# GEGLU feed-forward on one core: the head's first loads on one queue, ScalarE's table load ahead of its DMA

## The chip, the core and the metric

The kernel runs on one core of a Trainium2 chip. A core has five engines with their own instruction streams: TensorE (PE, matrix products), VectorE (DVE), ScalarE (ACT), GpSimd (POOL) and SyncE (SP, here only issuing DMAs). DMAs are issued by SP and by ACT, each onto a queue of its own; the packets of both queues run on the core's 16 DMA engines. The metric is device time in microseconds (us), median over runs.

## The reference

```python
B, S, D, F = 32, 32, 1024, 3584          # x: 1024 rows of 1024; all bfloat16
return (gelu(x @ w_gate) * (x @ w_up)) @ w_down      # gelu: tanh form
```

With the 32 x 32 rows flattened, x is 1024x1024, w_gate and w_up are 1024x3584 and w_down is 3584x1024.

## The kernel before

**The work.** Both layers are done with Strassen's scheme (seven products of half-size blocks in place of eight, in Winograd's form). In the first layer x is cut into two halves of rows (512 tokens each) and two halves of its 1024 inner columns; held transposed on the chip, these are the tiles `b11`, `b12`, `b21`, `b22`, each 128 partitions x 4 row blocks x 512 tokens. A row block is 128 of the inner dimension. The weights are cut likewise, and their sums (`s1` to `s4`, mostly on GpSimd) and the sums of x (`t1` to `t4`, on VectorE) feed the products. A main loop goes over 14 chunks of 256 columns of the gate and up weights; the second layer follows with the same scheme.

**The head.** Sums of weights and of x need many loads, so the kernel starts with products that need no sums: the second half of the gate's inner dimension (gate row blocks 4 to 7, called k = 0 to 3 here) times `b21`, for the first 24 column tiles. They come in groups of four column tiles, `a12_ahead[i]` (i = 0 to 5), 512 columns each; the first two groups are called `a12a`, the others `a12b`. TensorE's order here is written out by hand (`tc.manual_schedule()`), and each engine runs its instructions in that order:

1. six warm-up products on constants (line 256);
2. `transposed(0)`: x's first needed row block is loaded as it lies (`x_nat`), four TensorE transposes (line 264) turn it, and two VectorE copies (line 267) bring it into `b21` row block 0;
3. the products (line 284) of group i = 0 with k = 0, first half of the tokens, then `transposed(1)` for `b21` row block 1, then the second half of k = 0, and k = 1;
4. group i = 1 with k = 0 and 1 (eight products of 512 columns);
5. group i = 0 with k = 2 and 3, then group i = 1 with k = 2 and 3. `b21` row blocks 2 and 3 don't pass through TensorE: one transposing DMA from SP brings them (`load_xT(0, KD + KQ, DT)`, line 218). Then the groups i = 2, 3, 4 and so on.

**The loads that feed it**, in the order of their queues (line 197 is `load_nat`, one row block of x, 128 KB; line 211 is `load_ahead(i, k0, k1)`, row blocks k0 to k1 of group i, 128 KB each):

- SP: `x_nat` block 0; group 0, k = 0; group 0, k = 1; the transposing DMA; group 0, k = 2 and 3; group 1, k = 2 and 3; the halves of groups 2 and 3; the first chunk's weights; and more.
- ACT: `probe`, a fetch of 0.1 KB out of the gate rows of k = 0 and 1 (line 207); `x_nat` block 1; group 1, k = 0 and 1 (256 KB). Then ScalarE's first instruction that computes, a GELU on one column (line 248), which is preceded by the load of its function table. ScalarE then waits for the first products to copy out of PSUM.

**The completion counters.** The framework gives each DMA that SP or ACT issues one of eight completion semaphores, in turn, over both queues together, in the order in which the framework comes to the DMAs. A DMA that gets a semaphore that an earlier one holds carries a wait for that one's landing; the issuing engine stands at the instruction until then. In the kernel before, the eight semaphores go, in order, to `probe`, `x_nat` block 0, `x_nat` block 1, group 0 with k = 0, group 0 with k = 1, group 1 with k = 0 and 1, the transposing DMA, and group 0 with k = 2 and 3; SP's next DMA (group 1, k = 2 and 3) is the first with such a wait, for `probe`.

Of the kernel before, what the change touches and what calls it, by code (L numbers as in the profile page):

```python
# [13 lines left out]
def kernel(  # L14
# [20 lines left out]
    nc = tc.nc  # L35
    P = nc.NUM_PARTITIONS
    fp32 = mybir.dt.float32
    f32r = mybir.dt.float32r
    bf16 = mybir.dt.bfloat16
# [10 lines left out]
    KD = DT // 2  # L50
# [4 lines left out]
    KQ = DT // 4  # L55
# [8 lines left out]
    wg_r = w_gate.rearrange("(dt dp) f -> dp dt f", dp=P)  # L64
# [8 lines left out]
    xpool = one.enter_context(tc.tile_pool(name="x", bufs=1))  # L73
# [33 lines left out]
    def acc(tag):  # L107
        return ps1.tile([P, NB], fp32, name=f"ps{tag}", tag=tag, bufs=BANKS[tag])
# [82 lines left out]
    NB_P = NB // P  # L191
# [3 lines left out]
    with tc.manual_schedule():  # L195
        def load_nat(eng, dt, p0, p1):
            eng.dma_start(  # L197
                out=x_nat[:, p0:p1, dt * P : (dt + 1) * P],
                in_=xf[p0 * P : p1 * P, (KD + dt) * P : (KD + dt + 1) * P].rearrange("(b p) d -> p b d", p=P),
            )  # L200
# [1 line left out]
        assert KQ == 2  # L202
        load_nat(nc.sync, 0, 0, NB_P)


        probe = xpool.tile([P // 8, KQ, 2], bf16, name="probe")
        nc.scalar.dma_start(out=probe, in_=wg_r[::8, KD : KD + KQ, :2])

        def load_ahead(i, k0, k1, eng=nc.sync):
            f0 = i * KB  # L210
            eng.dma_start(
                out=a12_ahead[i][:, k0:k1, :],
                in_=wg_r[:, KD + k0 : KD + k1, f0 * P : (f0 + KB) * P],
            )

        def load_xT(nb, d0, d1):
            t = ((b11, b12), (b21, b22))[d0 // KD][nb]
            nc.sync.dma_start_transpose(
                out=t[:, d0 % KD : (d1 - 1) % KD + 1, :], in_=xf[nb * NB : (nb + 1) * NB, d0 * P : d1 * P]
            )  # L220

        load_ahead(0, 0, 1)
        load_nat(nc.scalar, 1, 0, NB_P)
        load_ahead(0, 1, 2)
        load_xT(0, KD + KQ, DT)
        load_ahead(1, 0, KQ, nc.scalar)
        a12_ahead += [spool.tile([P, KD, KB * P], bf16, name="a12b", tag=t) for t in ("s2", "s4", "s1", "s3")]
        for i in (0, 1):
            load_ahead(i, KQ, KD)
# [16 lines left out]
        def gelu(src, tag, bufs):  # L246
            h = ework.tile([P, NB], bf16, name=tag, tag=tag, bufs=bufs)[:, : src.shape[-1]]
            nc.scalar.activation(h, src, ACT.Gelu_apprx_tanh)  # L248
            return h


        gelu(ident[:, :1], "h0", 6)

        warm_ps = acc("A")
        for _ in range(NWARM):
# [363 lines left out]
```

## Time and profile before

| | |
|---|---|
| median of 3 runs | 274.18 us (273.29 to 275.09) |
| span of the profiled execution | 272.0 us (the page gives no other time of it; the median lies 2.2 us above) |
| PE busy | 267.1 us, 98% of the span |
| DVE, ACT, POOL busy | 201.2, 116.1, 119.3 us |
| PE on the chain of work that ended last | 97% |
| DMA on that chain | 1% |
| HBM traffic | 31.72 MB read, 2.10 MB written, 124 GB/s |

The span runs from the first to the last instruction; launch and end lie around it. A busy PE is not a PE at its peak, since matmuls are pipelined and their ends modelled; the chain of work that ended last tells more, because it is followed back from the last instruction through whatever released each step. Where the chain is PE alone, a delay of PE moves the end by as much; where another engine or a DMA is named, that wait is what a change there can shorten. The head is the first 10 us or so, and it is read from the timeline of that stretch: a row gives start, duration, engine (a `q` behind the engine's name marks the issue of a DMA), line, operation and tiles, and in brackets the idle time before it with what ended it. The list of DMA issues gives for each DMA the time from issue to landing.

### The profile page before, as it was taken

Reading aid. Unit: us, or ns where it says so; the run is one execution under the profiler, and the core shown is the slowest. Engines: PE = TensorE matmul, PEld = TensorE weight load, DVE = VectorE, ACT = ScalarE, POOL = GpSimd, SP = SyncE. Lnnn points to the kernel's source line nnn. Section 1 sums busy time; section 2 is a strip of 40 time slices with the busy share of each in tenths; the row PEclk is TensorE's granted clock in tenths of the full one; section 3 lists DMA queues with packets and bytes.
Section 4 is the critical chain, followed back from the end, with each engine's and each line's share of the span. In section 5 each row is a group of like instructions: output and inputs, shape, how many; then the busy total and the mean of one; then the engine's idle time right before and its main releaser. Section 6 shows DMA issues by size and latency. Waiting matters only on the chain.

```text
span 272.0 us, 3399 instructions
## 1 busy us (share of the span) xinstructions
PE 267.1 (98%) x1199; PEld 193.4 (71%) x1212; DVE 201.2 (74%) x205; ACT 116.1 (43%) x189; POOL 119.3 (44%) x60
## 2 busy tenths in 40 slices
PE   8999999999999999999999999999999999999995
PEld 4444776886787688688688687764458888888884
DVE  1448998886976876876787458569999999997721
ACT  2335865545644643645636535434000307770000
POOL 1090099976995994994995978000000000000000
PEclk9999999999999999999999999999999999999999
DMA  7999130504505505415234290005981437855111
GB/s 174 323 227 281 39 99 17 158 25 130 154 2 154 154 4 154 128 27 157 69 88 118 50 319 17 0 2 182 356 273 60 158 112 253 276 187 174 54 61 58
DMA packets 56048, 35.86 MB, mean 132 GB/s; under 512 B 9824, under 2 KB 56032, under 8 KB 56032
## 3 DMA queue, kind: packets, MB, share of 16 engines
q1 hardware_dynamic: 52736, 33.17, 42.6%
q10 hardware_dynamic: 3296, 2.49, 2.9%
q8 instruction: 9, 0.15, 0.2%
q14 instruction: 7, 0.06, 0.1%
HBM read 31.72 MB, written 2.10 MB: 124 GB/s over the span
## 4 chain that ended last, share of the span: by engine, by line
PE 97%; DMA 1%; issue 0%; SPq 0%; DVE 0%
PE psA L273 38%; PE psA L425 24%; PE psC L273 19%; PE psC L425 7%; PE psA L284 5%; PE psC L284 3%; PE psC L588 1%; DMA a12a<-in_w_gate_dram 1%; SPq L197 0%; PE tp L264 0%; DVE o_last L589 0%
## 5 line engine op out<-in xcount | busy, mean ns | idle before, releaser
L273 PE MATMUL psA<-t,s 128*128 128x512 f32 x224 | 57.2, 397 | 0.0
L248 ACT ACTIVATE h<-c 128x512 bf16<-128x512 f32 x56 | 34.6, 631 | 41.6 <-DVE c L303 41.6
L273 PEld LDWEIGHTS psA<-t,s 128*128 128x128 f32 x224 | 42.1, 188 | 9.5
L170 POOL TENSOR_TENSOR s<-wu 128x1024 fp32r<-128x1024 bf16 x13 | 28.8, 2215 | 32.9 <-DMA wu<-in_w_up_dram 27.9
L171 POOL TENSOR_TENSOR s<-s,wg 128x1024 fp32r<-128x1024 f32 x14 | 31.7, 2263 | 15.0 <-DVE s L170 14.0
L173 POOL TENSOR_TENSOR s<-wg,wu 128x1024 fp32r<-128x1024 bf16 x13 | 28.4, 2188 | 0.0
L273 PE MATMUL psA<-b,wg 128*128 128x512 bf16 x119 | 27.8, 379 | 0.6
L273 PE MATMUL psA<-t,a22r 128*128 128x512 f32 x112 | 27.9, 391 | 0.0
L273 PE MATMUL psC<-t,s 128*128 128x512 f32 x112 | 27.9, 391 | 0.0
L273 PE MATMUL psC<-b22r,s 128*128 128x512 f32 x112 | 27.6, 389 | 0.0
L303 DVE TENSOR_TENSOR c<-sn,psA 128x512 f32<-128x512 f32 x32 | 21.8, 682 | 6.7 <-PE psA L273 5.7
L308 ACT COPY sn<-psC 128x512 f32<-128x512 f32 x28 | 16.4, 590 | 20.9 <-PE psC L273 15.2
L273 PEld LDWEIGHTS psC<-t,s 128*128 128x128 f32 x112 | 21.0, 188 | 4.5
L273 PEld LDWEIGHTS psA<-t,a22r 128*128 128x128 f32 x112 | 21.0, 188 | 4.5
L273 PEld LDWEIGHTS psC<-b22r,s 128*128 128x128 f32 x112 | 21.0, 188 | 4.4
L303 DVE TENSOR_TENSOR c<-sn,psC 128x512 f32<-128x512 f32 x28 | 19.2, 688 | 6.5 <-PE psC L273 6.5
L273 PEld LDWEIGHTS <-wg 128*128 128x128 bf16 x128 | 11.8, 98 | 15.3 <-issue 2.4
L172 POOL TENSOR_TENSOR s<-wg,s 128x1024 fp32r<-128x1024 bf16 x10 | 21.6, 2158 | 0.8
L402 DVE TENSOR_TENSOR lo<-c,h 128x512 bf16<-128x512 f32 x14 | 20.4, 1459 | 0.9
L308 ACT COPY sn<-psA 128x512 f32<-128x512 f32 x32 | 18.4, 592 | 6.1 <-PE psA L273 6.0
L303 DVE TENSOR_TENSOR c<-ahead,psA 128x512 f32<-128x512 f32 x24 | 16.4, 687 | 4.0 <-PE psA L273 2.4
L321 DVE TENSOR_TENSOR hi<-h,psA 128x512 bf16<-128x512 bf16 x14 | 9.6, 688 | 12.4 <-PE psA L273 12.4
(85 smaller groups left out, 381.0 us busy)
## 6 DMA issues: line engine op xcount, KB each, us to landing
wu<-in_w_up_dram SPq DMA_DIRECT2D x14, 512.0 KB, 4.0
wdb<-in_w_down_dram SPq DMA_DIRECT2D x12, 512.0 KB, 4.9
wg<-in_w_gate_dram SPq DMA_DIRECT2D x9, 512.0 KB, 5.2
wdb<-in_w_down_dram SPq DMA_DIRECT2D x12, 384.0 KB, 4.5
v<-in_w_down_dram SPq DMA_DIRECT2D x4, 512.0 KB, 6.4
out_dram<-o_sb ACTq DMA_DIRECT2D x15, 128.0 KB, 1.7
wg<-in_w_gate_dram SPq DMA_DIRECT2D x6, 256.0 KB, 4.6
v<-in_w_down_dram SPq DMA_DIRECT2D x4, 384.0 KB, 7.5
```

The source lines that it names most:

```text
L170: yield engs[0].tensor_tensor(s1, a21, a22, ADD)
L171: yield engs[1].tensor_tensor(s2, s1, a11, SUB)
L172: yield engs[2].tensor_tensor(s4, a12, s2, SUB)
L173: yield engs[3].tensor_tensor(s3, a11, a21, SUB)
L248: nc.scalar.activation(h, src, ACT.Gelu_apprx_tanh)
L273: nc.tensor.matmul(ps, lhsT=lhs[:, k, :], rhs=rhs[:, k, :], start=(start and k == 0), stop=(k == KD - 1), skip_group_check=True,)
L284: nc.tensor.matmul(ps[:, cols], lhsT=a12_ahead[i][:, k, j * P : (j + 1) * P], rhs=b21[:, k, cols], start=(k == 0 and not cols.start), stop ...
L303: tt(t, s, ps, ADD)
L308: nc.scalar.copy(t, ps)
L321: tt(g_of(ft)[:, :NB], h0, psa, MUL)
L402: tt(g_of(ft)[:, NB:], added(sn5[fl], psa[fl]), h1[fl], MUL)
L425: nc.tensor.matmul(banks[m], lhsT=lhs(k)[:, m * P : (m + 1) * P], rhs=rhs(k), start=(start and k == 0), stop=(k == HF - 1), skip_group_che ...
```

## The change

The fetch of 0.1 KB goes. `x_nat` block 1 moves from ACT's queue to SP's, between the first two row blocks of group 0. The load of group 1, k = 0 and 1, stays on ACT's queue but is called after all of the head's other loads and after the one-column GELU, so that ScalarE loads its table and computes that column first.

```diff
         load_nat(nc.sync, 0, 0, NB_P)
 
-
-        probe = xpool.tile([P // 8, KQ, 2], bf16, name="probe")
-        nc.scalar.dma_start(out=probe, in_=wg_r[::8, KD : KD + KQ, :2])
-
         def load_ahead(i, k0, k1, eng=nc.sync):
...
         load_ahead(0, 0, 1)
-        load_nat(nc.scalar, 1, 0, NB_P)
+        load_nat(nc.sync, 1, 0, NB_P)
         load_ahead(0, 1, 2)
         load_xT(0, KD + KQ, DT)
-        load_ahead(1, 0, KQ, nc.scalar)
...
         gelu(ident[:, :1], "h0", 6)
+        load_ahead(1, 0, KQ, nc.scalar)
 
         warm_ps = acc("A")
```

## The prediction

> **What bounds the kernel now.** I read the chain of work that ended last first. Its shares say where a delay would reach the end, and its first pieces say what the head waits for.
>
> ```profile
> PE 97%; DMA 1%; issue 0%; SPq 0%; DVE 0%
> ```
>
> ```profile
> 0.74 0.45 SPq L197
> 1.19 0.06 issue
> 1.25 3.02 DMA a12a<-in_w_gate_dram
> 4.26 0.05 issue
> 4.31 0.61 PE psC L284 x2
> ```
>
> From 4.31 us on the chain names PE alone until the last store. The one DMA on it is the first gate row block (group 0, k = 0), issued at 1.25 and landed at 4.26. So whatever PE loses or gains in the head moves the end by as much, unless PE meets a new wait. The timeline of the first 10 us shows the issues and PE's order:
>
> ```profile
> 0.73 0.45 ACTq L207 DMA_DIRECT2D probe<-in_w_gate_dram  x1
> 1.21 0.49 ACTq L197 DMA_DIRECT2D x_nat<-in_x_dram  x1
> 1.25 1.03 SPq L211 DMA_DIRECT2D a12a<-in_w_gate_dram  x2
> 1.73 0.53 ACTq L211 DMA_DIRECT2D a12a<-in_w_gate_dram  x1
> 2.29 1.28 ACT L248 ACT_TABLE_LOAD   x1 [2.29 <-issue]
> 2.32 1.34 SPq L218 DMA_TRANSPOSE b<-in_x_dram  x1
> 3.75 0.51 DVE L267 COPY b<-tp 128x256 bf16<-128x256 bf16 x2 [3.75 <-PE tp L264]
> 4.31 0.61 PE L284 MATMUL psC<-b,a12a 128*128 128x256 bf16 x2 [0.39 <-DMA a12a<-in_w_gate_dram]
> 8.89 1.03 PE L284 MATMUL psC<-b,a12a 128*128 128x512 bf16 x4
> ```
>
> and the list of DMA issues, asked for one moment at a time, shows how long each took to land (last column, us):
>
> ```profile
> x_nat<-in_x_dram SPq DMA_DIRECT2D x1, 128.0 KB, 2.5
> x_nat<-in_x_dram ACTq DMA_DIRECT2D x1, 128.0 KB, 3.2
> a12a<-in_w_gate_dram ACTq DMA_DIRECT2D x1, 256.0 KB, 4.6
> b<-in_x_dram SPq DMA_TRANSPOSE x1, 4.9
> ```
>
> Added to the issue times these give landings: `x_nat` block 1 at 4.4, ACT's 256 KB (group 1, k = 0 and 1) at 6.3, the transposing DMA (`b21` blocks 2 and 3) at 7.2. The four 512-wide products that start at 8.89 are group 0 with k = 2. The eight before them are group 1 with k = 0 and 1, and eight such products take 1.73 (two chain pieces of the groups after them read 1.73 for x8); so group 1 starts at 8.89 - 1.73 = **7.17** (rounded up from 7.16), 0.9 after its weights have landed. That time is what the change touches.
>
> **Part 1: the moved row block and the dropped fetch.** SP issues one more DMA, at the pitch of its neighbours (two issues in 1.03, so 0.51 each). `x_nat` block 0 keeps 0.74 and group 0, k = 0, keeps 1.25; `x_nat` block 1 goes from 1.21 (ACT) to about 1.76, group 0, k = 1, from about 1.76 to 2.3, the transposing DMA from 2.32 to **2.83**, and everything behind it on SP goes 0.5 later. Group 0, k = 0, no longer shares the DMA engines with `x_nat` block 1. Its 3.0 can shrink to the 2.5 of the first `x_nat`, which is the same size with nothing ahead of it, so it would land at 3.75 to 4.26. PE can't use it before the first of the two copies at 3.75 is done, about 4.0, against 4.31 now. The gain is 0 to 0.3, and I take 0.25. PE then reaches group 1 at 6.92 instead of 7.17. `x_nat` block 1 lands at 4.3 to 5.0 (1.76 + 2.5 to 3.2); PE wants it after four quarter-size products, at about 4.9 as now, so it is hidden or nearly so. Group 0, k = 1, was waited for 0.25 (idle before PE's weight load at 6.28) and can only be earlier, with less beside it.
>
> The dropped fetch frees 0.45 of ScalarE's issue time and, by bytes, nothing of the DMA engines. Whether it readies the gate rows for the loads behind it no row shows. The bounds are 0 and, at worst, the spread between the quickest and slowest 128 KB loads of the head, 2.5 to 4.4 (the second load of the row at 1.25), so 1.9 on a load that PE waits for. I take 0, since a load with no fetch before it (`x_nat` block 0) is the quickest of all.
>
> **Part 2: the load that goes behind the table.** If ScalarE only had to do the table load and the GELU first (1.28 + 0.21, from 0.73 on), it would issue group 1's load at about 2.3 instead of 1.73, and with 3.2 to 4.6 to land, at 5.5 to 6.9, PE would not notice. But the built program of the changed kernel shows a wait on that instruction. On ScalarE and TensorE it reads (semaphore names in brackets):
>
> ```
> ACT 3  DMACopy a12a<-in_w_gate_dram 128x2x512 [waits DMAHW4]
> SP  5  DmaTransposeAnt b21<-in_x_dram 128x2x512
> PE 61  Ldweights a12a [waits DMAHW4]                (group 1, k = 0)
> PE 77  Ldweights a12a [waits DMAHW5]                (group 0, k = 2)
> PE 78  Matmult psC<-b21,a12a 128x512                (no DMA wait left)
> ```
>
> The eight completion semaphores are dealt out in turn. Called last, group 1's load comes to the fifth for the second time, and the fifth's first holder is SP's fifth DMA, the transposing one. PE's row 78 confirms it: it needs the transposed block, yet has no wait of its own, because row 61 has already waited for a later count of the same semaphore. Before, the same load held a fresh semaphore and waited for nothing, and row 78 did wait for the transposing DMA. So ScalarE stands until the transposing DMA lands, and only then issues a load that PE needs at 6.92. Behind ScalarE's instruction stand only copies that wait for PE's products anyway; behind PE's row 61 stands everything.
>
> The price, step by step. (a) The transposing DMA is issued at 2.83. With the 4.9 of its row it lands at 7.7. The lower end is from a later one of twice the rows:
>
> ```profile
> 19.21 3.65 SPq L218 DMA_TRANSPOSE b<-in_x_dram  x1
> ```
>
> ```profile
> b<-in_x_dram SPq DMA_TRANSPOSE x1, 5.7
> ```
>
> It landed 2.05 after its issue ended, so ours would land at 2.83 + 1.34 + 2.05 = 6.2. In the changed head 256 KB less runs beside it, so it should land earlier than in its own row; I take the middle, **6.9**. (b) The load itself, 256 KB on an empty queue beside a busy SP queue: at least the 2.5 of 128 KB with nothing ahead, at most the 5.3 that the last half of group 3 took on SP. Its own row says 4.6, standing behind `x_nat` block 1; `x_nat` block 1, half its size with only the small fetch ahead, says 3.2. I take 3.6. It lands at 6.9 + 0.05 + 3.6 = 10.55, and PE goes on at **10.6** (0.05 from a landing to PE, as at 4.26). (c) PE's delay is 10.6 - 7.17 = **3.4**; the bounds are 6.2 + 2.5 + 0.1 - 7.17 = 1.6 and 7.7 + 5.3 + 0.1 - 7.17 = 5.9. Part 1's 0.25 isn't taken off, since PE only arrives earlier at the same wait. (d) What is late next: group 0, k = 2 and 3, landed at 7.9, the weights of group 2 at 9.4 and 10.2; 0.5 later, all of these are still there by 10.6 or long before PE comes to them. The DMAs run on while PE stands, so nothing further holds it, but nothing gives the time back either, with PE alone on the chain.
>
> On the profiled span that is 272.0 + 3.4 = 275.4. The median lies 2.2 above the span, so the forecast is 274.18 + 3.4 = **277.6**.
>
> **Two rules.** In the Trainium skill, "DMA: Bandwidth & Descriptors", section "Issuing engines are not separate DMA queues", says that issuing from several engines only saves the sequencer's issue time. It speaks against any large effect of this change: by it the whole would cost SP's 0.5 of issue, and the sum would be 274.2. The rule knows nothing of a wait ahead of an issue.
>
> **PE's speed after the gap.** The warm-up products start 0.42 apart (six from 0.78, the last at 2.9), 512 columns each; 512-wide products after 7.17 come 0.22 apart. PE turns twice as fast at about 6, 5.1 after its first product, though the granted clock in the profile's rows reads 1.00 throughout. A gap of 10.6 - 6.92 = 3.7 may make it slow again: no cost if it stays fast, and at most another 5.1 at half speed, 2.6 lost. Nowhere after 6 does PE stand that long in this trace, so the row can't decide; I take 0, as the likelier, and keep both ends. The skill's "TensorE: Matmul & The Clock Gate", Part 1, says that one idle window of about 3.4 us brings the slow state back, with windows that run free of the kernel; this gap is about one window, and by the page's rule the price would be 0 or 1.7 to 3.4, an estimate from its window length at half speed.
>
> **The rivals.** A, the forecast: 277.6, or 276.1 to 279.0 with the nearer ends. B, the same wait and a slow PE behind it: 277.6 + 2.6 = 280.2. For it speaks the length of the gap, against it that it need not cover what the chip counts. C, not slower: the wait at ScalarE's issue is met before it matters, so that the load goes out at 2.3 and lands at 5.5 to 6.9, and only the 0.25 at 4.31 is left, 273.9. It decides if the issue goes out before about 3.3 (6.92 less 3.6); the listing speaks against it, since the transposing DMA landed at 7.2 even before. D, the load is quick, with both lower ends: 274.18 + 1.6 = 275.8. It is for a transposing DMA that was slow only through its neighbours.
>
> **How the numbers follow.** A 0.62, B 0.22, C 0.07, D 0.09. About 1% (2.7 us) is what a measurement of this kernel can tell from no change. Slower by more than that are B and most of A (a delay of 2.75 or more; I leave 0.10 of A below it): 0.74. Within it: C, D and that part of A, less a little: 0.25. Faster by over 1% would need a gain of ten times what the head's DMA wait holds: 0.01. The range from 275.9 to 280.5 takes in A and most of B and leaves out C, D's lower half and the upper tail of B, under 0.2 in all.
>
> **What would show it.** In the changed profile: ScalarE's table load at about 0.7; its 256 KB issue at about 7 and not 2.3; PE idle about 3.7 before its first weight load of group 1, put down to the DMA of `a12a`; the chain naming the transposing DMA, then ACT's issue, then that DMA, where it now names the one of 3.02; the rest of the span as long as before. First products at about 4.05 would show part 1. Warm-like pitches of 0.22 after the gap speak for A, 0.43 for B. I am wrong if the issue stands at 2.3, or if PE finds its weights there.

## The result and the profile after

The changed kernel takes 281.65 us (median of 6 runs, 280.63 to 282.11) against 274.05 us of the kernel before beside it (6 runs, 272.93 to 275.24): a ratio of 1.0277, 95% interval 1.0246 to 1.0308. It is slower, as forecast, but by 7.6 us where 3.4 were forecast, and outside the range.

The chain of work that ended last, of the changed kernel, by engine; before, DMA stood at 1%:

```profile
PE 95%; DMA 3%; SPq 1%; DVE 0%; issue 0%
```

Its pieces in the head (start, duration, what); before, the last wait on a DMA ended at 4.26:

```profile
2.79 3.35 DMA b<-in_x_dram
6.14 0.02 issue
6.16 5.82 DMA a12a<-in_w_gate_dram
11.98 0.04 issue
12.02 3.55 PE psA L280 x8
```

The transposing DMA (`b`) is issued by SP at 2.79 and lands at 6.14; 0.02 later ScalarE issues group 1's load, and that lands at 11.98. The timeline of the same stretch (start, duration, engine, line, operation; in brackets the idle time before it) shows the issue, PE's gap and what follows:

```profile
0.73 1.28 ACT L243 ACT_TABLE_LOAD   x1 [0.73 <-PEq L599]
2.03 0.21 ACT L243 ACTIVATE h<-ident 128x1 bf16<-128x1 bf16 x1
4.09 0.58 PE L280 MATMUL psC<-b,a12a 128*128 128x256 bf16 x2 [0.17 <-DVE b L263]
6.16 0.50 ACTq L207 DMA_DIRECT2D a12a<-in_w_gate_dram  x1
12.02 3.55 PE L280 MATMUL psA<-b,a12a 128*128 128x512 bf16 x8 [5.30 <-DMA a12a<-in_w_gate_dram]
15.41 1.03 PE L280 MATMUL psC<-b,a12a 128*128 128x512 bf16 x4
```

The first product of group 0 starts at 4.09 in place of 4.31: the small gain is there. ScalarE has its GELU done at 2.24 and issues nothing until 6.16. PE stands 5.30 and starts group 1 at 12.02 in place of 7.17. Its eight products then take 3.39 (12.02 to 15.41) in place of 1.73. The stretches of 2 us say why (columns: the stretch and its length; the busy time of PE, PEld (PE's weight loads), DVE, ACT and POOL, each with its instructions in brackets; the granted clock, that is, the share of full speed at which PE may run; the DMA share; GB/s):

```profile
10.00:12.00 2.00, 0.00 (x0) 0.00 (x0) 0.00 (x0) 0.00 (x0) 0.00 (x0) 1.00 1.06 350
12.00:14.00 2.00, 1.98 (x5) 0.73 (x6) 0.00 (x0) 0.00 (x0) 0.00 (x0) 0.50 1.17 323
14.00:16.00 2.00, 2.00 (x7) 0.75 (x6) 0.00 (x0) 0.00 (x0) 0.91 (x1) 0.65 1.30 316
16.00:18.00 2.00, 2.00 (x12) 0.88 (x9) 1.35 (x2) 1.41 (x3) 1.92 (x2) 1.00 1.11 226
```

The granted clock is 0.50 when PE comes back. So of the 6.7 us between the two spans (278.7 against 272.0), 12.02 - 7.17 = 4.85 are PE's later start and 3.39 - 1.73 = 1.66 are the slow products: 6.5 together. Behind the head nothing differs. The profiled execution, 280.63, is the shortest of the six; its mean granted clock is 0.993, and 0.987 or 0.988 in the other five, which is about twice as much time at half speed.

### The profile page after: what moved, and what is told of

Its sections match the earlier page's. It is cut to its first block, busy times and chain, and to the rows that moved or that the text cites. A ratio compares the mean times of both kernels' runs of the same rounds, so it can differ in the third digit from the quotient of the medians.

```text
span 278.7 us, 3412 instructions
## 1 busy us (share of the span) xinstructions
PE 269.4 (97%) x1212; PEld 193.8 (70%) x1212; DVE 202.3 (73%) x205; ACT 115.9 (42%) x189; POOL 119.8 (43%) x60
## 4 chain that ended last, share of the span: by engine, by line
PE 95%; DMA 3%; SPq 1%; DVE 0%; issue 0%
PE psA L269 37%; PE psA L421 24%; PE psC L269 18%; PE psC L421 7%; PE psA L280 5%; PE psC L280 2%; DMA a12a<-in_w_gate_dram 2%; DMA b<-in_x_dram 1%; PE psC L584 1%; SPq L207 0%; SPq L197 0%; DVE o_last L585 0%
## 5 line engine op out<-in xcount | busy, mean ns | idle before, releaser
L269 PE MATMUL psA<-b,wg 128*128 128x512 bf16 x128 | 29.4, 380 | 0.0
L269 PEld LDWEIGHTS <-wg 128*128 128x128 bf16 x128 | 11.8, 98 | 15.3 <-issue 2.4
L398 DVE TENSOR_TENSOR hi<-c,h 128x512 bf16<-128x512 f32 x14 | 17.3, 1238 | 0.9
```

The costliest lines, as they stand in the source:

```text
L269: nc.tensor.matmul(ps, lhsT=lhs[:, k, :], rhs=rhs[:, k, :], start=(start and k == 0), stop=(k == KD - 1), skip_group_check=True,)
L398: tt(g_of(ft)[:, NB:], added(sn5[fl], psa[fl]), h1[fl], MUL)
```

## The experiments

Theory **W**: the cost is the wait of group 1's load for the transposing DMA, which the shared completion semaphore makes, and what follows from it. Rival **M**: the moved row block or the dropped fetch costs by itself. Theory **H**, on top of W: PE's gap turns its clock down, and that is a part of the loss of its own. Later came **Q** and **Q2**, on why the load took 5.82 to land. All ratios are to the kernel before, run beside the experiment.

### The wait taken away, first try

```diff
-        gelu(ident[:, :1], "h0", 6)
+        gelu(ones_m[:, :1], "h0", 6)
```

> The changed kernel with the source of ScalarE's one-column GELU taken from the constant ones in place of the identity that GpSimd builds; its result is used nowhere. ScalarE's order stays (table load, GELU, then the load of group 1), but the built program gives the load a semaphore that no earlier DMA holds, so it has no wait. Theory W (the wait for the transposing DMA is the cost): issue at about 2.3 in place of 6.16, landing at 5.5 to 6.9, no idle PE between 6.7 and 12.0, the clock fast from its first rise on; 273.8 to 274.3 us, 0.973 of the changed kernel. Theory M (the moved row block, or the dropped fetch, is the cost): 281 to 282 us, as the changed kernel.

Measured: 275.42 us, ratio 1.0038 (1.0011 to 1.0065). Nearly all of the loss is gone, which M doesn't allow; but the time is 1.1 us above W's highest figure. The timeline shows that this kernel isn't W's kernel:

```profile
0.73 1.28 ACT L243 ACT_TABLE_LOAD   x1 [0.73 <-PEq L599]
0.79 0.48 ACTq L207 DMA_DIRECT2D a12a<-in_w_gate_dram  x1
4.19 0.61 PE L260 MATMUL tp<-ident,x_nat 128*128 128x128 bf16 x4 [0.70 <-DMA x_nat<-in_x_dram]
```

With no wait between them, ScalarE issued the load at 0.79, while its table load, which stands ahead of it in its order, was still running. So the 256 KB moved beside x's first row block, which PE got at 4.19 in place of 3.30.

### The load ahead of the table

```diff
         load_xT(0, KD + KQ, DT)
+        load_ahead(1, 0, KQ, nc.scalar)
...
         gelu(ident[:, :1], "h0", 6)
-        load_ahead(1, 0, KQ, nc.scalar)
```

> The changed kernel with the load of group 1 called where it was before, so that ScalarE issues it at about 0.7, ahead of its table load; x's second row block stays on SyncE's queue and the small fetch stays out. Theory W: no wait, landing by 5 us at the latest, 273.8 to 274.3 us. Theory M: 281 to 282 us. Were it only the place behind the table that costs, without the wait, this one would be fast and the kernel with the GELU on ones slow.

Measured: 275.73 us, ratio 1.0057 (1.003 to 1.0085). Again most of the loss is gone and 1 to 2 us are left, in the same place: the chain begins

```profile
0.73 3.73 DMA x_nat<-in_x_dram
```

with x's first row block landing at 4.46 beside the early load.

### The move of the load alone

```diff
-        load_ahead(1, 0, KQ, nc.scalar)
...
         gelu(ident[:, :1], "h0", 6)
+        load_ahead(1, 0, KQ, nc.scalar)
```

(in the kernel before; the small fetch and x's second row block stay on ScalarE's queue)

> The kernel before with only the load of group 1 called after the GELU; the small fetch and x's second row block stay on ScalarE's queue. The built program makes the load wait for the transposing DMA, as in the changed kernel. Theory W: the transposing DMA lands at about 6.5 to 7.2, the load is issued then, and PE stands until about 11 to 13; 280 to 283 us. Theory M: 274 us. On the load's own 5.8 us in the changed kernel: if they came from its being the first DMA on ScalarE's queue, here, with two DMAs ahead of it on that queue, it lands 3.6 to 4.6 after its issue; if they came from SyncE's busy queue, it takes 5 to 6 again.

Measured: 281.66 us, ratio 1.026 (1.0213 to 1.0306), the whole loss, as W says, with both other parts undone. Its chain:

```profile
2.24 3.97 DMA b<-in_x_dram
6.23 6.30 DMA a12a<-in_w_gate_dram
12.57 3.60 PE psA L284 x8
```

The load took 6.30 with two DMAs ahead of it on the same queue, so the 5.82 of the changed kernel were not those of a queue used for the first time.

### PE kept busy in the gap

```diff
+    NFILL = 23
...
+        for _ in range(NFILL):
+            nc.tensor.matmul(ps[1][0], lhsT=ones_w, rhs=ones_m, start=True, stop=True, skip_group_check=True)
         for j in range(KB):
             product_ahead(ps[1][j], 1, j, 0, KQ)
```

> The changed kernel with 23 products of constants, 512 columns each, put in TensorE's order ahead of group 1's first product; the bank that they write is cleared by that product. At 0.216 us each they take 5.0 us, nearly all of the 5.3 that PE stands. Theory H (the gap turns PE's clock down, and that is the part of the loss beyond the gap itself): the wait stays, PE goes on at about 12.0, the granted clock stays at 1.00 after its first rise, and the eight products after the gap start 0.22 apart in place of 0.43; 1.7 to 2.7 us less than the changed kernel, 279.0 to 280.0 us. If the slow products are due to something else that ends at 15.4, such as the DMAs beside them, the time stays at 281 to 282 us.

Measured: 279.8 us (4 runs, 279.32 to 281.96), ratio 1.0229 (1.0173 to 1.0285). In the profiled run the mean granted clock is 1.000, and the eight products behind the wait run at full speed (two of the other three runs have 1.000 as well; the longest, 281.96, has 0.994, so in that one the filling did not keep PE fast):

```profile
12.56 1.90 PE L281 MATMUL psA<-b,a12a 128*128 128x512 bf16 x8
14.30 1.03 PE L281 MATMUL psC<-b,a12a 128*128 128x512 bf16 x4
```

14.30 - 12.56 = 1.74, where the changed kernel took 3.39 for them, beside nearly the same DMA traffic (316 GB/s from 12 to 14 us, there 323). H holds in the profile: the gap is what slows them. The load landed 0.5 later here, so of the 1.66 only 1.2 show in the span (277.5 against 278.7). The medians differ by 1.85, but the two intervals overlap, so the size rests on the profiles.

### The wait taken away, second try

```diff
-        gelu(ident[:, :1], "h0", 6)
+        nc.scalar.activation(a12_ahead[1][:, 0, :1], ones_m[:, :1], ACT.Gelu_apprx_tanh)
         load_ahead(1, 0, KQ, nc.scalar)
```

> The changed kernel with the one-column GELU reading the constant ones and writing into the tile that group 1's load fills (the load overwrites it), so that the load truly waits for the GELU and for nothing else: no earlier DMA holds its semaphore. This is the changed order of the loads without the wait for the transposing DMA and without the issue at 0.79 that the kernel with the GELU on ones showed. Theory W: issue at about 2.25, landing at 5.5 to 6.9, x's first row block landed at 3.1 to 3.3, first product of group 0 at about 4.1, no PE idle of more than 0.3 behind it; 273.3 to 274.0 us against 273.7 to 274.1 of the kernel before, ratio 0.997 to 1.000. If the moved row block or the dropped fetch cost something by themselves (theory M in a small form, for which the 275.4 and 275.7 of the last two kernels could speak), 275 to 276 us again.

Measured: 274.55 us, 0.55 above the expected range, ratio 1.0005 (0.998 to 1.0031). This is the change in all its parts but the wait for the transposing DMA (the one-column GELU has another source and target), and nothing of the loss is left; nor is there a gain.

```profile
2.27 0.45 ACTq L207 DMA_DIRECT2D a12a<-in_w_gate_dram  x1
4.09 0.59 PE L280 MATMUL psC<-b,a12a 128*128 128x256 bf16 x2 [0.17 <-DVE b L263]
6.26 0.39 PE L280 MATMUL psC<-b,a12a 128*128 128x256 bf16 x2 [0.52 <-DMA a12a<-in_w_gate_dram]
8.87 1.03 PE L280 MATMUL psC<-b,a12a 128*128 128x512 bf16 x4
```

The 0.22 won at 4.09 is spent at 6.26 on the second gate row block, which moves beside the load here, as it does in the kernel before; group 0 with k = 2 starts at 8.87, before at 8.89. The expected "no idle of more than 0.3" was wrong.

### All on one queue

```diff
         load_ahead(0, 1, 2)
+        load_ahead(1, 0, KQ)
...
-        load_ahead(1, 0, KQ, nc.scalar)
```

> The changed kernel with group 1's load on SyncE's queue too, ahead of the transposing DMA; ScalarE issues no load at all. Theory Q (packets of two busy queues stall each other: between 8 and 10 us the kernel before moved 350 GB/s on one queue, the changed one 263 on two, with single 1 KB packets up to 1.15 us long): with one queue hardly a packet over 0.2 us between 2 and 9 us, the load lands 2.5 to 3.5 after an issue at 2.8, the transposing DMA, issued at 3.4, by 7.2, group 0 with k = 2 and 3 by 8.2, and PE waits for none of them; 273.2 to 273.9 us. Rival: the DMA engines are simply full, the load takes 4 to 5 and the transposing DMA lands at 8 or later, and PE waits for group 0 with k = 2 and 3; 274.5 to 275.5 us.

Measured: 275.01 us, ratio 1.003 (1.0003 to 1.0057). The rival has the time and the wait right: PE waits for group 0 with k = 2, and for group 1 before it. Its landings were a little late: the load took 3.9 (2.79 to 6.67), and the transposing DMA landed at 7.68.

```profile
6.71 1.90 PE L280 MATMUL psA<-b,a12a 128*128 128x512 bf16 x8 [0.49 <-DMA a12a<-in_w_gate_dram]
9.52 1.04 PE L280 MATMUL psC<-b,a12a 128*128 128x512 bf16 x4 [0.91 <-DMA a12a<-in_w_gate_dram]
```

Theory Q's forecast fails too: with SP's queue alone the trace still has 32 packets of over 0.2 us between 2 and 9 us, the longest 1.18, and the stretch from 6 to 8 us moved 234 GB/s against the changed kernel's 279. The stretch that Q had started from, 8 to 10 us, moved 343 GB/s here against the changed kernel's 263, which is as Q would have it; but the changed kernel moved 262 from 8 to 9 already, and no packet of ScalarE's load had run by then (the first is at 9.0). What stalls single packets, and what slowed that stretch, stays open.

### The other two parts, each alone in the kernel before

```diff
-        probe = xpool.tile([P // 8, KQ, 2], bf16, name="probe")
-        nc.scalar.dma_start(out=probe, in_=wg_r[::8, KD : KD + KQ, :2])
```

> The kernel before without its fetch of 0.1 KB, nothing else changed: ScalarE's two loads go out 0.48 earlier, at 0.73 and 1.22. Theory S (the fetch acts as a spacer: what ScalarE issues at 0.73 takes DMA engine time from x's first row block, which PE waits for): x's first row block lands at 3.6 to 4.2 in place of 3.26, and the time is 0.4 to 1.0 above the kernel before, 274.2 to 275.0 us. Theory R (the fetch readies the gate rows): x's first row block lands as before, and the first gate row block and group 1's load land later than their 4.26 and 6.3. Neither: 273.7 to 274.1 us.

Measured: 273.82 us, ratio 1.0003 (0.997 to 1.0037). In the profile x's first row block is late, as S says, and PE starts on it at 3.87 in place of 3.30:

```profile
3.87 0.61 PE L262 MATMUL tp<-ident,x_nat 128*128 128x128 bf16 x4 [0.38 <-DMA x_nat<-in_x_dram]
```

The time doesn't show it. Its interval leaves room for about 1 us either way, so how much the fetch is worth stays open. On the scale of the 7.6 us lost by the change, dropping it costs nothing.

```diff
-        load_nat(nc.scalar, 1, 0, NB_P)
+        load_nat(nc.sync, 1, 0, NB_P)
```

> The kernel before with x's second row block on SyncE's queue, nothing else changed: ScalarE issues the small fetch at 0.73 and group 1's load at 1.21, whose packets come from about 2.4 on. x's first row block lands at 3.2 to 3.3 as before; group 1's load competes with the first gate row block and x's second one, which land at about 4.0 to 4.5 and 4.5 to 5.2; PE wants the second one at 4.9. Theory W gives the move itself 0 to 0.4 us: 273.7 to 274.5. Theory M (the moved row block costs by itself): 275 us or more.

Measured: 274.96 us, ratio 1.0041 (1.0004 to 1.0077): between the figures of the two theories. PE waits 0.35 for that row block at 5.44, since group 1's load, one place further up on ScalarE's queue, moves beside it:

```profile
5.44 0.43 PE L264 MATMUL tp<-ident,x_nat 128*128 128x128 bf16 x4 [0.35 <-DMA x_nat<-in_x_dram]
```

### Why the load took 5.8

```diff
         gelu(ident[:, :1], "h0", 6)
+        nc.scalar.copy(a12_ahead[1][:, 0, :1], b21[:, KQ, :1])
         load_ahead(1, 0, KQ, nc.scalar)
+        nc.scalar.copy(a12_ahead[2][:, 0, :1], a12_ahead[1][:, 0, :1])
```

(cut short: the GELU and the load themselves also move up, so that these four lines stand ahead of the loads of group 2)

> The changed kernel in which the load of group 1 waits for the transposing DMA through data (a one-column copy of what that DMA brings, into the tile that the load overwrites), and SyncE's queue is held behind its seventh DMA until that load has landed (a one-column copy out of the loaded tile into group 2's tile, which SyncE's next load overwrites). The load is issued at 6.3 to 6.6 as in the changed kernel, but beside it only the 512 KB that SyncE issued between 4.2 and 5.3 are left to move. Theory Q2 (the 5.8 to 6.3 that this load took are time spent behind what SyncE's queue keeps issuing): it lands within 3.0 to 4.2 of its issue, at 9.5 to 10.7, and PE goes on 1.3 to 2.5 earlier than 12.0. Rival (it is the lateness, or the first use of ScalarE's queue, whatever runs beside): 5.5 to 6.3 again. The time itself is 279.5 to 281 us by Q2, if the loads held back are not wanted before they land, and 282 or more by the rival.

Measured: 278.73 us, ratio 1.0161 (1.0121 to 1.0202). The load's row in the list of DMA issues (KB, us to landing), first of the changed kernel, then of this one:

```profile
a12a<-in_w_gate_dram ACTq DMA_DIRECT2D x1, 256.0 KB, 5.8
```

```profile
a12a<-in_w_gate_dram ACTq DMA_DIRECT2D x1, 256.0 KB, 3.4
```

Q2 holds: issued as late, at 6.56, but with SP's queue held behind its seventh DMA, the load lands 3.4 after its issue. In the changed kernel the trace shows no packet of this load before 9.00, so 2.84 of the 5.82 passed ahead of its first packet; here the first one runs at 7.72, 1.16 after the issue. PE goes on at 10.11 in place of 12.02, and the kernel is quicker than the changed one, by 2.9 us in the medians and 1.6 in the profiled spans (277.1 against 278.7), although SP's later loads all start after 10.2. The time is below the 279.5 to 281 that Q2 had expected.

## Why the prediction was wrong

**What bounds the kernel** was read rightly: PE alone carries the chain behind the head, and a PE delay of 6.5 in the head moved the span by 6.7.

**Part 1** came as worked out: SP's issues stand at 1.24, 1.77, 2.24 and 2.79 (forecast 1.25, 1.76, 2.3, 2.83), the first product at 4.09 (4.05). That this gain leads nowhere, because PE only waits longer at group 1, was right too. Costed at nothing, the dropped fetch and the moved row block are together nothing when the load goes out at 2.27; each changes the head a little, by when the load comes to move beside x's row blocks.

**Part 2's mechanism** is shown. The load goes out 0.02 after the transposing DMA lands, as the program's listing has it; with the move alone that wait makes the whole loss (1.026), and with the change whole but the wait gone none is left (1.0005). Rival C is out, and D with it.

**The terms of the sum** are where it failed. (a) The transposing DMA lands at 6.14, 3.35 after its issue; I had 6.9. The lower end, 6.2, was the right one: 2.01 from the end of the issue to the landing, where the later row had 2.05. That error made the forecast longer by 0.8. (b) The load took 5.82; I had 3.6, with 5.3 as the end. This is the first step that failed. I had placed it between two rows whose DMAs went out by 1.73, when SP had issued two of 128 KB and was at its third. At 6.16 SP had issued four DMAs of 256 KB since 4.18 and went on with two more and the up weights, and the load's first packet ran at 9.00, its others beside what SP had still in flight; with SP held at the second of the four the load took 3.4, close to what I had taken. (c) So PE went on at 12.02 in place of 10.6, a delay of 4.85 in place of 3.4.

**PE's speed after the gap** is the second step that failed. I took 0 and gave rival B a chance of 0.22. B is what happened: the gap of 5.3 brought half speed at 12.0. In size B's 2.6 was too much for the profiled run, 1.66, as the slow stretch lasts 3.4 there and not 5.1. The rule quoted beside it, from the Trainium skill's "TensorE: Matmul & The Clock Gate", Part 1, agrees with the trace: one window of about 3.4 at half speed, from 12.0 to 15.4, is its lower figure of 1.7. The row of this case could not decide, and then a gap that I put at 3.7 should not have counted as harmless.

Either error alone would have stayed within the range: 274.18 + 4.85 = 279.0 for the delay, 277.6 + 1.66 = 279.3 for the clock. Together they make 274.18 + 6.5 = 280.7, which is the profiled run's 280.63. The median's further 1.0 goes with the lower mean clock of the other five runs. That is inferred from the means, since only the shortest was profiled. A profile of such a run exists for the kernel with the move of the load alone (mean clock 0.988): the granted clock is 0.50 from before PE's return at 12.57 until about 17.2, the eleven products until then lose 2.3, and with the delay of 12.57 - 7.17 = 5.4 that makes the 7.7 by which its span, 279.7, exceeds 272.0.

The rule on queues, that issuing from several engines only saves issue time, would have given 274.2. For the changed order of the loads without the wait it holds (ratio 1.0005). The skill's "DMA: Bandwidth & Descriptors", section "Issuing engines are not separate DMA queues", also says that DMAs of all engines interleave on the same 16 DMA engines. The 3.4 against 5.8 agrees with the sharing, which I had left out of (b); that half of the 5.8 passed before the load's first packet is more than the sentence says.

## What to carry to other kernels

A load that is called later, or that stands behind a compute instruction, may be given a completion semaphore that an earlier DMA still holds; list the waits of the built program, name the DMA that each waits for, and price the load from its landing. Price a DMA that is issued late by what the other queue has in flight then, not by the time that the same DMA took at the start. A gap in TensorE's work of the size of those here (3.68, 5.30 and 6.30 us all brought half speed; 0.91 did not, and nothing between was measured) is to be priced twice: as itself, and as products at half speed behind it.

## What the runs showed that I had not expected

- ScalarE issues a DMA while an earlier table load on the same engine is still running: at 0.79, inside a table load of 0.73 to 2.01. "Table first" alone therefore delays a load by nothing; in the changed kernel only the wait did.
- PE can turn slow after it has come back. With SP's queue held, PE went on at 10.11 after 3.68 idle, ran fast at first, and its weight loads stood 0.43 apart only from about 11.8 on:

```profile
11.84 0.15 PEld L280 LDWEIGHTS <-a12a 128*128 128x128 bf16 x1 [0.28 <-issue]
12.26 0.15 PEld L280 LDWEIGHTS <-a12a 128*128 128x128 bf16 x1 [0.28 <-issue]
12.69 0.15 PEld L280 LDWEIGHTS <-a12a 128*128 128x128 bf16 x1 [0.28 <-issue]
```

- The first rise of PE's speed comes at a different time in each execution. With the GELU on ones, products of 256 columns stood 0.21 apart until 8.3; with the load ahead of the table, they stood 0.11 apart from the first, at 5.18. That is worth up to about 1.5 us of span, so differences of less than that between two profiles are read from the waits and not from the spans.
- The place of a DMA in the semaphores' turn is the framework's and not to be read off the order of the calls. Between the changed kernel and the first try only the source of the GELU differs, yet the load waited until 6.14 in the one and went out at 0.79, with no wait, in the other.
